# A constant guard column in the softmax's scores, with other due times for the planner

## The chip, the cores and the metric

One core of a Trainium2 chip runs the whole program in one launch. The metric is device time in microseconds (us), the median of several runs. TensorE (PE in the profile) multiplies matrices, VectorE (DVE), ScalarE (ACT) and GpSimd (POOL) work on tiles in on-chip memory, and SyncE (SP) issues nearly all the transfers (DMAs).

## The reference

What is computed is local attention followed by two layers of products. Cut to what matters:

```python
# attention: B=2, H=8, S=768, D=64; window of 16 to either side, and 24 summaries of 32 keys each
k_sum = k.reshape(B, H, nb, block, D).max(axis=3)
v_sum = v.reshape(B, H, nb, block, D).mean(axis=3)
scores_all = concat([where(|i - j| < 16, scale * q k^T, -1e9), scale * q k_sum^T + log(32)])
scores_all = scores_all - max(scores_all)
a = exp(scores_all)
a = a / (sum(a) + 1e-09)
x = a @ concat([v, v_sum])                      # 1536 x 512
h = ((x @ w1) * (x @ w2)) @ w3 @ w_out          # 1536 x 512
u = h @ w_in                                    # 1536 x 2048
y = (u * clip(u + 3, 0, 6) / 6) @ w_out2        # 1536 x 512
```

The addition of 1e-09 to the sum is the guard that the title speaks of.

## The kernel before, in words

**The products.** Every 32-bit operand is split into a high and a low part (`to_hi_lo`, lines 296 to 306: ACT writes the high part in line 301, POOL or DVE the low part in line 304), and a product is three matmuls (`products`, line 347): high by high, low by high, high by low. The weights arrive as 64-bit numbers; `to_f32` (lines 255 to 294) makes 32-bit ones of them with two operations on ACT or one on ACT and one on DVE (lines 277, 283, 288) and one more on DVE (line 292). `convert` (line 308) does both for one block of weights and numbers its calls; for the numbers in `LO_DVE` the low part is made on DVE, for all others on POOL. It is called 24 times for W' = w3 w_out (`wprime`: numbers 0 and 1 for the first step, 2 and 3 for the second, up to 15; then 16 to 23) and 16 times for w1 and w2 (numbers 24 to 39). Later weights go through `convert_out` and `w_in_group`, which count on but don't look at `LO_DVE`.

**The attention.** Queries are handled in 12 units u of two tiles of 64 queries each. `probabilities(u)` loads the queries, takes the scores on PE (line 483), and then: two DVE operations scale them and add the mask into the tile `sc` (line 493, 128 partitions, 8 groups of 120 scores each); DVE takes the maximum of each group into `st` (line 507); POOL subtracts it (line 509); ACT takes the exponential over all 960 elements (line 510); DVE sums each group (line 513), adds 1e-9 (line 514) and takes the reciprocal (line 515); POOL multiplies by it (line 519). `attend(u)` transposes the result on PE (line 529), copies it out, multiplies by the values on PE (line 544) and splits the result for the products. Units 0 to 3 make up the first block of 512 tokens; they read keys that stay on the chip (`kres`), and the summaries of the keys (`ksum`, three reductions on DVE, line 364) and of the values (`vsum`, three on DVE, line 400). The four transposes of `vsum` (`vsum_rows`, line 426) need the constants `con` for their identity matrix and go through bank 7 of the accumulator, which ACT empties (line 431); the scores of unit 0 use banks 6 and 7 after that.

**The order.** Nothing is issued in program order. Each piece of work is entered in `Graph` with its engine, an assumed duration and a due time. `schedule` first works the due times backwards: that of a PE operation is the least of its own and of what its users need, and that of an operation on any other engine comes from its users alone (its own is not read):

```python
due = [o[2] if o[0] == "pe" else self.LAST for o in self.ops]
for i in range(n - 1, -1, -1):
    for u in users[i]:
        e = self.ops[i][0]
        due[i] = min(due[i], due[u] - self.ops[i][1] - self.LAT.get(e, 40))
```

Then it runs a list schedule with the assumed durations: an engine that is free takes the ready operation that is due first. The result is a fixed order for each engine's queue. `slack` delays when the users of an operation count as ready, and `begin` when the operation itself may start. The constants on lines 157 to 172 feed this: `DUE_W` and `DUE_Q` for PE's W' products and attention units, `DUE_ROWS` for the transposes of `vsum`, `DUE_FF` for the start T1 of the main products, `AHEAD` for how far the later attention units stand ahead of them, `HOLD` for the slack of the late weights, `OUT_AT` for when the late weights may begin to load.

**The late stage.** From about the middle on, weights of the last layer are combined, spilled to DRAM (line 318) and fetched again (lines 322, 985, 1034), all by SP's queue; ACT copies results out of the accumulator (line 855).

Of the kernel before, what the change touches and what calls it, by code (L numbers as in the profile page):

```python
# [22 lines left out]
F32 = mybir.dt.float32  # L23
# [3 lines left out]
AF = mybir.ActivationFunctionType  # L27
ALU = mybir.AluOpType
AX = mybir.AxisListType

P = 128
# [9 lines left out]
NK = NWIN + NSUM  # L41
KW = 2 * QT + 2 * WIN
KS = KW + 2 * NSUM
NPAIR = H // 2
# [109 lines left out]

DUE_W = ((77.78, -6.43), (102.28, 1.95))
DUE_K, DUE_V, DUE_ROWS = 121.82, -109.4, 7.92
DUE_Q = (307.31, 41.78)
V_AT = 1  # L160
LO_DVE = [2, 9, 15, 16, 17, 18, 22, 26, 28, 29, 30, 31, 32, 36, 38, 42, 44, 45, 47]
L3_ACT = [2, 3, 4, 5, 6, 7, 8, 10, 11, 12, 15, 17, 18, 20, 22, 23, 24]
DUE_FF = 30.71
AHEAD, BEHIND = -16.03, -118.65
SUMS_AT, SUMS_DUE = 3, 5.0
POOL_MAX = ()
HOLD = 3512.7
SUMS_LATER = 22839.1
OUT_LATER = 31254.19
IN_AT = (8, 12)  # L170
LAST_ORDER = (0, 1, 4, 5, 2, 3, 6, 7)
OUT_AT, OUT_STEP = 174.13, 5.88


def build(tc, qd, kw, vw, kt, vt, consts, wp_in, w12_in, w2_in, out):
    nc = tc.nc
    g = Graph()
    us = 1000.0
# [4 lines left out]
    pool = main.__enter__()  # L183
# [13 lines left out]
    bank = [pp.tile([P, TB], F32, name=f"bank{i}") for i in range(8)]  # L197
# [7 lines left out]
    att = att_cm.__enter__()  # L205
    kall = [att.tile([P, NPAIR, KS], F32, name=f"kall{i}") for i in range(2)]
    vall = [att.tile([P, DM], F32, name=f"vall{i}") for i in range(4)]
    qst = [att.tile([P, 2, NPAIR, QT], F32, name=f"qst{i}") for i in range(2)]
    sc = [att.tile([P, 2, NPAIR, NK], F32, name=f"sc{i}") for i in range(2)]
    pt = [att.tile([P, NPAIR * P], F32, name=f"pt{i}") for i in range(2)]  # L210
    st = [att.tile([P, 3, 2 * NPAIR], F32, name=f"st{i}") for i in range(2)]
    con = att.tile([P, 4 * NK + P], F32, name="con")
# [2 lines left out]
    ident = con[:, 4 * NK :]  # L215
# [140 lines left out]

    load(0, lambda: con, consts, P * (4 * NK + P) * 4, ["con"])
    g.op("pool", 60, 0, lambda: nc.gpsimd.memset(three, 3.0), (), ["three"])


    def max32(due, x, c, reads):
# [88 lines left out]
    def probabilities(u, due, bk):  # L450
        i2, uu = u % 2, u % PPB
        ki, si, sti, qs = kall[i2], sc[i2], st[i2], qst[i2]
# [36 lines left out]
        for x in range(2):  # L489
            m = (0 if uu == 0 else 1) if x == 0 else (3 if uu == PPB - 1 else 2)  # L490
            g.op(
                "dve", 660, due + 1 * us,
                lambda x=x, m=m: nc.vector.scalar_tensor_tensor(  # L493
                    out=si[:, x], in0=bank[bk[x]][:, 0 : NPAIR * NK].rearrange("p (a n) -> p a n", a=NPAIR),
                    scalar=SCALE, in1=con[:, m * NK : (m + 1) * NK].unsqueeze(1).to_broadcast((P, NPAIR, NK)),
                    op0=ALU.mult, op1=ALU.add,
                ), [("bank", bk[x]), "con"], [("s", i2, x)],
            )
        s8 = si.rearrange("p x a n -> p (x a) n")
        s1 = si.rearrange("p x a n -> p (x a n)")  # L500
        skeys = [("s", i2, 0), ("s", i2, 1)]

        def wide(k):
# [3 lines left out]
             lambda: nc.vector.tensor_reduce(out=sti[:, 0, :], in_=s8, op=ALU.max, axis=AX.X), skeys, [("st", i2)])  # L507
        g.op("pool", 2000, due + 3 * us,
             lambda: nc.gpsimd.tensor_tensor(out=s8, in0=s8, in1=wide(0), op=ALU.subtract), [("st", i2)], skeys)  # L509
        g.op("act", 1020, due + 4 * us, lambda: nc.scalar.activation(out=s1, in_=s1, func=AF.Exp), [], skeys)  # L510

        def inv():
            nc.vector.tensor_reduce(out=sti[:, 2, :], in_=s8, op=ALU.add, axis=AX.X)
            nc.vector.tensor_scalar(out=sti[:, 0, :], in0=sti[:, 2, :], scalar1=1e-9, scalar2=None, op0=ALU.add)
            nc.vector.reciprocal(out=sti[:, 1, :], in_=sti[:, 0, :])  # L515

        g.op("dve", 1560, due + 5 * us, inv, skeys, [("st", i2)])
        g.op("pool", 2000, due + 5.5 * us,
             lambda: nc.gpsimd.tensor_tensor(out=s8, in0=s8, in1=wide(1), op=ALU.mult), [("st", i2)], skeys)  # L519

    def attend(u, due, b0, b1):
        i2 = u % 2
        j, col = u // PPK, (u % PPK) * 2 * QT
        s0 = A_X + NPAIR * j
        si, vi, bk = sc[i2], [2 * i2, 2 * i2 + 1], (b0, b1)

        def trans(x):
            for p in range(NPAIR):
                nc.tensor.transpose(bank[bk[x]][0:NK, p * P : (p + 1) * P], si[:, x, p, :], ident)  # L529

        for x in range(2):
            g.op("pe", 480, due + 7 * us, lambda x=x: trans(x), [("s", i2, x), "con"], [("bank", bk[x])])
# [148 lines left out]
    with tc.manual_schedule():  # L681
        first_k(DUE_K * us)
        for n in range(2 * NFC):
            if n < NFC:
                wprime(0, n, (DUE_W[0][0] + DUE_W[0][1] * n) * us)
            else:
                wprime(1, n - NFC, (DUE_W[1][0] + DUE_W[1][1] * (n - NFC)) * us)
            if n == V_AT:
# [9 lines left out]
        for u in range(PPK):  # L698
            at = (DUE_Q[0] + DUE_Q[1] * u) * us
            probabilities(u, at, (6, 7))  # L700
# [26 lines left out]
        due = T1  # L727
        pend = None
        for j in range(NBLK):
            for n_i in range(NFC):  # L730
                i = LAST_ORDER[n_i] if j == NBLK - 1 else n_i
# [284 lines left out]
        for n, store, i, hh, bks, start in LAST:  # L1016
            last = n == LAST[-1][0]
            done = []
            for k in range(NFC):
                b11, b21, b12, b22 = held(k), moved(0, 1, k), moved(1, 0, k), moved(1, 1, k)  # L1020
                other = (lambda k=k: tmps[6 + k % 2]), ("f", 6 + k % 2)
                o, x, y = {
                    1: (b11, None, None), 2: (b21, None, None), 3: (b22, None, None),
                    5: (b11, b12, b11), 6: (b11, b22, b11), 7: (other, b22, b12), 4: (other, b21, b11),
                }[n]
                if x:
                    tensors(due, o[0], x[0], y[0], ALU.subtract, x[1], y[1], o[1], "dve")
                s = t_ring[n_t % len(t_ring)]
# [6 lines left out]
                         out=slot(ws)[:, wh, :].bitcast(F32).rearrange("p (two n) -> p two n", two=2),  # L1035
                         in_=d[:, :, hh * H : (hh + 1) * H]),
                     [(store, 2 * k + i)], [("t", ws, wh)])
                done.append((s, ws, wh))
                for m in range(2):
                    if last and k >= NFC - 3:  # L1040
                        continue
                    terms = [(lambda a, ws=ws, wh=wh, m=m: slot(ws)[:, wh, a * H + m * P : a * H + (m + 1) * P],
                              lambda c, s=s: slot(s)[:, c, :])]
# [3 lines left out]
            for m in range(2):  # L1047
                if last:
                    for s, ws, wh in done[NFC - 3 :]:
                        terms = [(lambda a, ws=ws, wh=wh, m=m: slot(ws)[:, wh, a * H + m * P : a * H + (m + 1) * P],  # L1050
                                  lambda c, s=s: slot(s)[:, c, :])]
# [91 lines left out]
```

## Time and profile before

| | |
|---|---|
| median of 3 runs | 557.11 us (555.17 to 557.39) |
| the profiled execution | 555.27 us |
| its span, first to last instruction | 553.5 us |
| PE busy in it | 526.9 us (95%) |
| DVE, ACT, POOL busy | 375.7, 303.5, 289.2 us |
| mean granted TensorE clock | 0.99 |

A row of a timeline gives start, duration, engine, line, operation and tiles, and in brackets how long the engine had been idle before it and what ended that. The chain of waits follows the work that ended last back to the start. "x32" is a number of instructions merged in one row.

### The profile page before, as it was taken

What the parts mean: (1) busy time and instruction counts of PE and PEld (TensorE: products, weight loads), DVE (VectorE), ACT (ScalarE), POOL (GpSimd) and SP (SyncE); (2) the same over time, 40 slices, a digit from 0 to 9 for tenths busy, and PEclk for the clock granted to TensorE, in tenths of its full rate; (3) what the DMA queues carried; (4) which work ended last, traced back from release to release, by engine and by line L of the source; (5) the groups of instructions that cost most, each with busy time, mean ns of one, the idle gap of its engine ahead of it and who ended that gap; (6) DMA issues with size and microseconds to landing.
All of it is one profiled execution on the core that took longest, in us unless ns stands there. A gap on an engine that the chain in (4) does not pass through costs nothing.

```text
span 553.5 us, 8514 instructions
## 1 busy us (share of the span) xinstructions
PE 526.9 (95%) x3112; PEld 431.4 (78%) x3112; DVE 375.7 (68%) x460; ACT 303.5 (55%) x517; POOL 289.2 (52%) x239
## 2 busy tenths in 40 slices
PE   0399999999999999999999999999999999999997
PEld 0388788888788888888888888888888887888875
DVE  5889978578463447777553866577775569689941
ACT  0879876484232446564545786655663456734630
POOL 0668454673221334374728665875785563644630
PEclk9789999999999999999999999999999999999999
DMA  8999678662241368633347576475444679877631
GB/s 318 363 364 336 197 245 261 187 195 62 65 123 53 121 215 270 218 115 115 114 157 229 222 247 209 156 263 172 150 174 142 209 264 366 294 256 231 190 103 75
DMA packets 54513, 111.32 MB, mean 201 GB/s; under 512 B 4792, under 2 KB 26296, under 8 KB 54472
## 3 DMA queue, kind: packets, MB, share of 16 engines
q1 hardware_dynamic: 54472, 110.79, 59.9%
q8 instruction: 24, 0.39, 0.3%
q14 instruction: 17, 0.14, 0.1%
HBM read 84.26 MB, written 26.21 MB: 200 GB/s over the span
## 4 chain that ended last, share of the span: by engine, by line
PE 91%; DMA 4%; DVE 1%; SPq 1%; POOL 1%; issue 0%; ACT 0%; ACTq 0%; DVEq 0%
PE bank L347 84%; PE bank L544 2%; PE bank L483 2%; PE bank L529 2%; DMA con<-in_con_dram 2%; DMA ws<-arena 1%; DMA w<-wo 1%; SPq L249 1%; DMA gj<-tg 1%; DVE sc L493 0%; POOL sc L519 0%; POOL sc L509 0%; SPq L1034 0%; PE bank L426 0%; DVE st L507 0%
## 5 line engine op out<-in xcount | busy, mean ns | idle before, releaser
L347 PE MATMUL bank<-arena,w 128*128 128x512 f32 x1152 | 268.3, 390 | 1.2 <-ACT late_f L855 1.2
L347 PEld LDWEIGHTS bank<-arena,w 128*128 128x128 f32 x1152 | 215.4, 188 | 47.2 <-ACT late_f L855 2.4
L347 PE MATMUL bank<-arena 128*128 128x512 f32 x960 | 230.9, 394 | 0.0
L347 PEld LDWEIGHTS bank<-arena 128*128 128x128 f32 x960 | 178.8, 189 | 38.2 <-issue 0.8
L292 DVE SCALAR_TENSOR_TENSOR c<-c,raw 128x512 uint32<-128x512 uint32 x48 | 47.7, 1006 | 22.2 <-ACT raw L283 17.5
L301 ACT ACTIVATE arena<-late_f 128x512 fp32r<-128x512 f32 x64 | 39.5, 628 | 39.2 <-DVE late_f L770 16.8
L304 POOL TENSOR_TENSOR w<-c,w 128x512 fp32r<-128x512 f32 x29 | 44.0, 1525 | 24.4 <-ACT w L301 24.3
L304 DVE TENSOR_TENSOR arena<-late_f,arena 128x512 fp32r<-128x512 f32 x44 | 39.6, 901 | 20.5 <-ACT arena L301 20.2
L826 POOL TENSOR_TENSOR late_f<-arena 128x512 f32<-128x512 f32 x16 | 23.2, 1447 | 44.7 <-DMA arena<-wo 30.4
L304 POOL TENSOR_TENSOR arena<-late_f,arena 128x512 fp32r<-128x512 f32 x20 | 29.5, 1476 | 32.0 <-ACT arena L301 26.5
L277 ACT ACTIVATE c<-raw 128x512 f32<-128x512 f32 x48 | 31.6, 663 | 25.2 <-DMA raw<-in_w_dram 24.3
L283 ACT ACTIVATE raw<-raw 128x512 uint32<-128x512 uint32 (+1 forms) x66 | 42.9, 655 | 0.0
L598 DVE TENSOR_TENSOR tg<-ta,bank 128x512 f32<-128x512 f32 x24 | 16.5, 685 | 38.8 <-PE bank L347 33.0
L304 POOL TENSOR_TENSOR raw<-c,raw 128x512 fp32r<-128x512 f32 x16 | 21.7, 1360 | 40.3 <-ACT raw L301 38.8
L509 POOL TENSOR_TENSOR sc<-sc,st 128x960 f32<-128x960 f32 x12 | 23.5, 1957 | 31.5 <-DVE st L507 31.5
L579 DVE TENSOR_TENSOR arena<-tg,arena 128x512 fp32r<-128x512 f32 x36 | 34.4, 955 | 5.4 <-ACT arena L574 4.8
L304 POOL TENSOR_TENSOR arena<-c,arena 128x512 fp32r<-128x512 f32 (+1 forms) x22 | 27.0, 1243 | 20.6 <-ACT arena L301 20.5
L574 ACT ACTIVATE arena<-tg 128x512 fp32r<-128x512 f32 x40 | 25.2, 629 | 20.1 <-DVE tg L598 16.6
L874 DVE SCALAR_TENSOR_TENSOR late_f<-ta,late_f 128x512 f32<-128x512 f32 x24 | 28.9, 1204 | 6.7 <-ACT ta L871 6.3
L770 DVE TENSOR_TENSOR late_f<-arena,late_f 128x512 f32<-128x512 f32 x24 | 29.1, 1242 | 6.2 <-DMA arena<-gj 6.1
L301 ACT ACTIVATE w<-c 128x512 fp32r<-128x512 f32 x40 | 24.6, 625 | 14.8 <-POOL c L770 6.5
L519 POOL TENSOR_TENSOR sc<-sc,st 128x960 f32<-128x960 f32 x12 | 22.0, 1832 | 17.0 <-DVE st L515 16.6
(68 smaller groups left out, 553.4 us busy)
## 6 DMA issues: line engine op xcount, KB each, us to landing
raw<-in_w_dram SPq DMA_DIRECT2D x48, 512.0 KB, 4.7
raw<-in_wp_dram SPq DMA_DIRECT2D x22, 512.0 KB, 6.0
wo<-raw SPq DMA_DIRECT2D x16, 512.0 KB, 3.4
arena<-wo SPq DMA_DIRECT2D x16, 512.0 KB, 3.3
ws<-arena SPq DMA_DIRECT2D x16, 512.0 KB, 3.4
w<-ws SPq DMA_DIRECT2D x32, 256.0 KB, 4.0
arena<-gj SPq DMA_DIRECT2D x24, 256.0 KB, 4.5
w<-wo SPq DMA_DIRECT2D x24, 256.0 KB, 4.0
```

The costliest lines, as they stand in the source:

```text
L277: lambda uf=uf, wf=wf: nc.scalar.activation(out=uf, in_=wf[:, :, 1], func=AF.Prelu, scale=2.0**-112, alpha=-(2.0**32)),
L283: lambda lw=lw: nc.scalar.activation(out=lw, in_=lw, func=AF.Copy, scale=2.0**-29 * (1 - eps), bias=7.5 * eps - 0.5),
L292: lambda ci=ci, ui=ui, lw=lw: nc.vector.scalar_tensor_tensor(out=ci, in0=ui, scalar=3, in1=lw, op0=ALU.logical_shift_left, op1=ALU.bitwise ...
L301: lambda: nc.scalar.activation(out=hi(), in_=src(), func=AF.Copy), keys, khi)
L304: lambda: e.tensor_tensor(out=lo(), in0=src(), in1=hi().bitcast(F32), op=ALU.subtract),
L347: nc.tensor.matmul(out=out_ap, lhsT=lhs(a), rhs=rhs(c), start=start and n == 0, stop=stop and n == 3 * len(terms) - 1, skip_group_check=skip,)
L509: lambda: nc.gpsimd.tensor_tensor(out=s8, in0=s8, in1=wide(0), op=ALU.subtract), [("st", i2)], skeys)
L574: g.op("act", 630, due, lambda: nc.scalar.activation(out=slot(s)[:, 0, :], in_=src_ap, func=AF.Copy), [src_key], [("t", s, 0)])
L579: lambda: eng.tensor_tensor(out=slot(s)[:, 1, :], in0=src_ap, in1=slot(s)[:, 0, :].bitcast(F32), op=ALU.subtract), [src_key, ("t", s, 0)], ...
L770: lambda: e.tensor_tensor(out=out(), in0=a(), in1=b(), op=op), [ka, kb], [ko], True)
L826: lambda i=i, s=s: nc.gpsimd.tensor_tensor(out=tmps[6 + i], in0=f32s(s, 0)(), in1=f32s(s, 1)(), op=ALU.add), both(s), [k])
L874: lambda: nc.vector.scalar_tensor_tensor(out=dst(), in0=t, scalar=6.0, in1=h(), op0=ALU.min, op1=ALU.mult),
```

## The change

The score tile gets a 121st column in each group. It is set to 1e-9 once for each of the two buffers by POOL, before any unit, and no later operation writes it. Scaling, maximum, subtraction, exponential and multiplication work on the first 120 columns; the sum takes all 121, and so holds the guard already. The separate addition goes. The exponential, which ran over 960 elements in a row, now runs over 8 groups of 120 with a gap of one. The assumed duration of the sum and reciprocal falls from 1560 to 1420 ns. The planner's constants change too.

```diff
-DUE_W = ((77.78, -6.43), (102.28, 1.95))
-DUE_K, DUE_V, DUE_ROWS = 121.82, -109.4, 7.92
-DUE_Q = (307.31, 41.78)
+DUE_W = ((77.78, -6.43), (139.42, 1.95))
+DUE_K, DUE_V, DUE_ROWS = 121.82, -109.4, -31.56
+DUE_Q = (309.83, 41.78)
-LO_DVE = [2, 9, 15, 16, 17, 18, 22, 26, 28, 29, 30, 31, 32, 36, 38, 42, 44, 45, 47]
+LO_DVE = [9, 13, 16, 17, 18, 22, 26, 28, 29, 30, 31, 32, 38, 42, 44, 47]
-DUE_FF = 30.71
-AHEAD, BEHIND = -16.03, -118.65
+DUE_FF = 31.07
+AHEAD, BEHIND = -15.06, -118.65
-HOLD = 3512.7
+HOLD = 3470.14
-OUT_LATER = 31254.19
+OUT_LATER = 33015.51
-OUT_AT, OUT_STEP = 174.13, 5.88
+OUT_AT, OUT_STEP = 174.69, 5.88
...
-    sc = [att.tile([P, 2, NPAIR, NK], F32, name=f"sc{i}") for i in range(2)]
+    sc = [att.tile([P, 2, NPAIR, NK + 1], F32, name=f"sc{i}") for i in range(2)]
...
+    for i in range(2):
+        g.op("pool", 60, 0,
+             lambda i=i: nc.gpsimd.memset(sc[i].rearrange("p x a n -> p (x a) n")[:, :, NK : NK + 1], 1e-9),
+             (), [("s", i, x) for x in range(2)])
...
-        s8 = si.rearrange("p x a n -> p (x a) n")
-        s1 = si.rearrange("p x a n -> p (x a n)")
+        all8 = si.rearrange("p x a n -> p (x a) n")
+        s8 = all8[:, :, 0:NK]
...
-        g.op("act", 1020, due + 4 * us, lambda: nc.scalar.activation(out=s1, in_=s1, func=AF.Exp), [], skeys)
+        g.op("act", 1020, due + 4 * us, lambda: nc.scalar.activation(out=s8, in_=s8, func=AF.Exp), [], skeys)
...
-            nc.vector.tensor_reduce(out=sti[:, 2, :], in_=s8, op=ALU.add, axis=AX.X)
-            nc.vector.tensor_scalar(out=sti[:, 0, :], in0=sti[:, 2, :], scalar1=1e-9, scalar2=None, op0=ALU.add)
-            nc.vector.reciprocal(out=sti[:, 1, :], in_=sti[:, 0, :])
-        g.op("dve", 1560, due + 5 * us, inv, skeys, [("st", i2)])
+            nc.vector.tensor_reduce(out=sti[:, 2, :], in_=all8, op=ALU.add, axis=AX.X)
+            nc.vector.reciprocal(out=sti[:, 1, :], in_=sti[:, 2, :])
+        g.op("dve", 1420, due + 5 * us, inv, skeys, [("st", i2)])
```

In `probabilities` and `attend` the writes of the scores (line 493) and the reads of the transposes (line 529) name the first 120 columns in the same way.

## Rows read from the trace of the kernel before

**Rows 1.** The page's first part: busy time, share of the span, instructions of each engine.
```profile
PE 526.9 (95%) x3112; PEld 431.4 (78%) x3112; DVE 375.7 (68%) x460; ACT 303.5 (55%) x517; POOL 289.2 (52%) x239
```

**Rows 2.** The waits of PE: engine, line, released by, us in total, times, longest.
```profile
PE bank L426 <- DMA con<-in_con_dram: 13.1, 1, 13.1
PE bank L529 <- POOL sc L519: 7.0, 1, 7.0
PE bank L483 <- DVE sc L493: 1.3, 1, 1.3
PE bank L347 <- ACT late_f L855: 1.2, 1, 1.2
```

**Rows 3.** Windows: stretch, its length, busy us (count) by engine, PE's clock, DMA share, GB/s.
```profile
19.81:26.84 7.03, 0.00 (x1) 0.00 (x1) 6.37 (x11) 6.98 (x13) 5.84 (x5) 0.54 0.98 327
26.84:32.16 5.32, 5.32 (x47) 4.50 (x47) 4.09 (x7) 3.23 (x6) 5.16 (x4) 0.65 1.02 397
```

**Rows 4.** The chain of waits: start, us, what. Its beginning, and two late pieces.
```profile
4.27 8.65 DMA con<-in_con_dram
...
13.05 1.03 PE bank L426 x4
14.10 0.60 ACT vall L431
14.74 2.24 PE bank L483 x34
...
24.34 0.31 POOL arena L304
...
24.99 1.80 POOL sc L519
...
454.17 6.22 DMA ws<-arena
...
461.64 54.74 PE bank L347 x240
```

**Rows 5.** The timeline of SP's queue in the first 5 us: the order of the loads.
```profile
0.73 0.86 SPq L249 DMA_DIRECT2D raw<-in_vt_dram  x2
1.64 0.65 SPq L249 DMA_DIRECT2D kres<-in_kt_dram  x1
2.33 0.61 SPq L249 DMA_DIRECT2D raw<-in_vt_dram  x1
2.98 1.24 SPq L249 DMA_DIRECT2D kres<-in_kt_dram  x2
4.27 0.91 SPq L249 DMA_DIRECT2D con<-in_con_dram  x1
```

**Rows 6.** The timeline of DVE: the last key reduction, and unit 0's guard and reciprocal.
```profile
12.17 1.22 DVE L364 TENSOR_REDUCE ksum<-kres 128x32 f32<-128x1024 f32 x1 [0.25 <-DMA kres<-in_kt_dram]
...
24.16 0.20 DVE L514 TENSOR_SCALAR st<-st 128x8 f32<-128x8 f32 x1
24.40 0.20 DVE L515 RECIPROCAL st<-st 128x8 f32<-128x8 f32 x1
```

**Rows 7.** The guard's own line, all 12: duration ns least/median/most, first and last start.
```profile
L514 DVE TENSOR_SCALAR st<-st x12: 171/188/1184, 24.2 to 232.3; 128x8 f32<-128x8 f32 x12
```

**Rows 8.** Groups by line and form: POOL additions on 512 elements, flat and strided.
```profile
L304 POOL TENSOR_TENSOR arena<-c,arena 128x512 fp32r<-128x512 f32 x18 | 24.2, 1356 | 18.4 <-ACT arena L301 18.3
L378 POOL TENSOR_TENSOR raw<-raw 128x512 f32<-128x512 f32 x3 | 4.7, 1570 | 0.1
```

**Rows 9.** The timeline of POOL where the last W' blocks of the first half are split.
```profile
51.32 2.54 POOL L304 TENSOR_TENSOR arena<-c,arena 128x512 fp32r<-128x512 f32 x2
53.82 2.24 POOL L509 TENSOR_TENSOR sc<-sc,st 128x960 f32<-128x960 f32 x1
62.59 1.30 POOL L304 TENSOR_TENSOR arena<-c,arena 128x512 fp32r<-128x512 f32 x1 [6.53 <-ACT arena L301]
```

**Rows 10.** The timeline of SP's queue ahead of the late spill.
```profile
450.25 3.56 SPq L985 DMA_DIRECT2D arena<-gj  x5
```

More of the change, by code (lines that the diff above doesn't have):

```diff
@@ L493, in probabilities @@
                 lambda x=x, m=m: nc.vector.scalar_tensor_tensor(
-                    out=si[:, x], in0=bank[bk[x]][:, 0 : NPAIR * NK].rearrange("p (a n) -> p a n", a=NPAIR),
+                    out=si[:, x, :, 0:NK], in0=bank[bk[x]][:, 0 : NPAIR * NK].rearrange("p (a n) -> p a n", a=NPAIR),
                     scalar=SCALE, in1=con[:, m * NK : (m + 1) * NK].unsqueeze(1).to_broadcast((P, NPAIR, NK)),
@@ L528, in trans @@
             for p in range(NPAIR):
-                nc.tensor.transpose(bank[bk[x]][0:NK, p * P : (p + 1) * P], si[:, x, p, :], ident)
+                nc.tensor.transpose(bank[bk[x]][0:NK, p * P : (p + 1) * P], si[:, x, p, 0:NK], ident)
         for x in range(2):
```

## The prediction

> **What bounds the kernel now.** I began with the busy line of the page: PE is busy for 526.9 of 553.5 us [rows 1], so at most 26.6 us can be had without giving PE less to do, and the change takes nothing from PE. Next the waits of PE, which say where those 26.6 us are: 13.1 until the constants have landed, 7.0 until unit 0's softmax is done, 1.3 in between, and 1.2 once late, on a copy by ACT [rows 2]. They make 22.8; the rest is mostly the end, after the last matmul. So PE stops only ahead of 26.84 us and once near 461 us. Between these it works without a gap, and an operation of DVE or POOL there costs or saves nothing until it is late enough to stop PE. The reader should see from this that 11 of the 12 softmaxes are hidden: only unit 0's is on the path.
>
> Then the windows around the first softmax: in 19.81 to 26.84 PE runs nothing and its granted clock averages 0.54, that is, it has dropped to its lower level (1.2 GHz); in the next 5.32 us it averages 0.65 [rows 3]. Beginning earlier by a fraction of a microsecond leaves such a pause and its slow restart as they are, so the stretch behind it moves as a whole. Last, the chain of waits through the start [rows 4], and the queues that feed it [rows 5, 6].
>
> **Start: the order of the loads.** A PE operation's due time counts, and others take theirs from their users. The planner's backward pass gives the transposes of `vsum` an inherited due time of -6.43 us before the change (arithmetic of the listing, no time of the chip), so their own 7.92 didn't count. The new -31.56 does, and with it the three V loads and `con` become due before the keys' loads. The queue now has V, V, K, V, K, K, con [rows 5]; I expect V, V, V, con, K, K, K. It is the same set of bytes, so the last of the seven should land when `con` does now, at 4.27 + 8.65 = 12.92 [rows 4]. Before, what followed was transposes from 13.05 (1.03), ACT's copy from 14.10 (0.60), scores at 14.74 [rows 4]. After, the transposes and the copy run while the keys still arrive, and the last key load is followed by one reduction of 1.22 [rows 6] alone: 12.92 + 1.22 = 14.14, scores at about 14.19 with the hand-over. Gain 14.74 - 14.19 = 0.55 us. The ends: if the last key block still landed for a reduction at 12.17 [rows 6], the scores could start at 13.39 + 0.05, a gain of 1.3; if it came one reduction (1.22) later than I say, a loss of 0.67. I take 0.55, the value that the bytes give.
>
> **Unit 0's softmax: the guard goes.** From the start of the guard to the start of the reciprocal are 24.40 - 24.16 = 0.24 us [rows 6]. That would be the gain if POOL were waiting. It isn't: a low part (line 304) stands in its queue in front of the multiplication and the multiplication starts at 24.99 [rows 4], 0.39 us after the reciprocal's end at 24.60. I count the 0.24 as covered: 0. If the planner puts that low part behind the multiplication, POOL starts at 24.36 and the gain is 24.99 - 24.36 = 0.63. The assumed duration falls by only 0.14, so I keep the order as it is and 0.63 for the range.
>
> **The other eleven guards.** They take 0.17 to 1.18 us each [rows 7], some six times the shortest at worst. Under the PE work of the middle they are hidden; gain 0. It is a reserve for DVE, not time.
>
> **The 121st column.** The sum takes 8 more elements of 968; at the 1.22 us of 1024 elements [rows 6] that is 10 ns. POOL's two passes and ACT's exponential now walk rows 121 apart. No row shows this form. The nearest pair: POOL on 512 elements takes 1356 ns flat and 1570 strided, with groups of 16 out of 32 [rows 8], 16% more. On unit 0's path one POOL pass of 1.80 [rows 4] would then gain 0.28, two 0.57; the lower end is 0, since the broadcast operand made POOL walk 8 rows already. A gain is excluded, as no element is saved. I take 0: rows of 120 with a gap of one are much nearer to flat.
>
> The Trainium skill speaks against this column: in "SBUF — State Buffer", section "Door 1: The DMA port swizzle", it says that this memory has lines of 16 bytes and each access that crosses to a new line pays. Rows of 480 bytes begin on a line; of those of 484 only every fourth does, and the other 120-element rows touch 31 lines in place of 30. By that rule a pass of 1.80 grows by 0.06 at most, two by 0.12, and the sum below would be -0.43 where I have -0.55; no row here shows lines.
>
> **Two memsets** of 8 elements on POOL at the very start: what waits for them follows the first scores, which end at 14.74 + 2.24 = 16.98 [rows 4]. Cost 0; without that cover I would put them at 0.2 each, an estimate from DVE's 0.20 for 8 elements [rows 6].
>
> **Low parts that change engines.** Only numbers up to 39 are looked up, so what changes is 2, 15 and 36 from DVE to POOL and 13 from POOL to DVE. One costs POOL 1.36 us [rows 8]. Number 2 falls in a stretch in which POOL works 5.16 of 5.32 us [rows 3]; queued behind it is unit 1's multiplication, which PE needs only after several W' products. Number 15 falls behind the pair at 51.32 and ahead of unit 3's subtraction (2.24), after which POOL is idle for 6.53 us [rows 9]; number 13, which POOL loses in front of it, pays for it. Number 36 falls where PE has long blocks ahead. Each 0; without cover number 15 would hold PE by up to 1.36.
>
> **The other constants.** The second W' due time and `DUE_Q` stand later than what their users ask for, before and after: nothing. `OUT_LATER` goes to no PE operation and isn't read. T1 moves by 0.36 with everything behind it; `AHEAD` puts the later units 0.97 us earlier against the products, which PE does back to back in either order. `OUT_AT` and `HOLD` let the late weights load 0.5 us later. What this could touch is the late wait of 1.2 us [rows 2]. Ends: the wait gone (-1.2), or the slower rival below. I take 0.
>
> **The sum**: -0.55 + 0 = -0.55 us. The profiled execution took 555.27 (span 553.5 and 1.77 around it), which would become 554.7. The median of the runs shown is 557.11, 1.84 above the profiled one; I forecast the median: 557.11 - 0.55 = 556.6. A measurement of this kernel can tell about 0.5%, 2.8 us, from no change.
>
> **The rivals.** (a) *The load order changes nothing.* The chain has other steps that wait for weights: DVE and ACT take weight operations between unit 0's steps, and if these hold the softmax at the same time as before, an earlier start of the scores is lost in front of them. For it: the DMA share is 0.98 up to 26.84 [rows 3]; against it: unit 0's steps in the chain follow each other closely. This is also the case in which the planner doesn't move the loads. Time 557.1.
>
> (b) *Faster: PE's 7.0 us are filled.* If the new plan lets the first W' products run before unit 0's transposes, 12 matmuls leave the path behind. At 54.74 / 240 = 0.228 us each [rows 4] that is 2.7, with the load order 3.3: 553.8. Against it: the last low part of the first step comes on POOL only behind unit 0's multiplication, and a shorter softmax makes the transposes earlier still.
>
> (c) *Slower: the late hand-over.* PE's wait near 461 us ends a chain through a spill that takes 454.17 to 460.39 [rows 4] and that SP issues behind five fetches, whose issue alone takes 3.56 us [rows 10]. If the shifted late weights make the planner put five more fetches ahead of that spill, it lands 3.56 later, the slot comes free later, and PE, which has no cover there (it waits already), stands for all of it: 557.11 - 0.55 + 3.56 = 560.1. It decides from 3.35 us on, at 559.9. For it: the queue is full of fetches of nearly the same due time. Against it: the shift is 0.5 us, less than one of these.
>
> **How the numbers follow.** The forecast has 0.53: the start gains something, the rest holds. Its own range is from -1.3 - 0.63 - 1.2 = -3.1 (554.0) to +0.67 + 0.57 = +1.2 (558.3). (a) has 0.20, within it. (b) has 0.13, (c) 0.14. Faster by over 0.5% (below 554.3) is (b) and a little of the low end of the forecast, 0.17; slower (above 559.9) is (c), 0.14; no difference 0.69. The range goes from just under (b), 553.5, to 559.4, short of (c).
>
> **What would show it.** Right: SP issues V, V, V, con, K, K, K; PE's first wait ends well before 13 us and another small one, on the keys' reduction, stands before the scores; scores begin near 14.2; unit 0's transposes begin at 26.3 in place of 26.84; PE busy unchanged; line 514 gone and DVE's total less by some 5 us. Wrong: a new wait of PE between 27 and 440 us (POOL low parts too late, above all number 15), a late wait other than 1.2, POOL's two passes of unit 0 over 1.80, or PE products before unit 0's transposes.

## The result: 0.5% slower, by loads that stand behind a waiting queue entry

The changed kernel took 559.31 us (median of 8 runs, 557.43 to 561.63), the kernel before 556.70 beside it (8 runs, 554.88 to 557.86): a ratio of 1.0051, with a 95% interval of 1.0029 to 1.0074. I had forecast 556.6, a small gain. The time lies in the range given, 0.1 us from its upper end of 559.4, but its sign is the other one. That it lies there is luck: no term of the range stood for what took the time, and a second measurement of the same kernel, e8 below, gives 560.20. The profiled execution took 558.5 us, its span 556.7, 3.2 longer than before.

The page's busy line answers [rows 1], and PE's waits answer [rows 2]:

```profile
PE 527.8 (95%) x3112; PEld 431.7 (78%) x3112; DVE 369.6 (66%) x446; ACT 301.3 (54%) x517; POOL 290.5 (52%) x243
```

```profile
PE bank L430 <- DVE vsum L404: 8.5, 1, 8.5
PE bank L532 <- POOL sc L522: 7.3, 2, 6.8
PE bank L487 <- DMA qst<-in_q_dram: 5.9, 2, 3.8
PE bank L347 <- ACT late_f L858: 2.0, 2, 1.5
PE bank L532 <- DVE sc L497: 1.4, 1, 1.4
```

DVE lost 6.1 us of work and the time did not fall: the guards were hidden. The start is cut up in another way: 8.5 + 6.8 + 5.9 = 21.2 us of waits, where it had 13.1 + 7.0 + 1.3 = 21.4. New are 1.4 us for the scores of line 497, a second wait of 0.5 (7.3 less 6.8) for line 522, and a second one for `late_f`.

**The start** changed in its order as forecast, and gained nothing. SP's queue (compare [rows 5]):

```profile
0.74 1.34 SPq L249 DMA_DIRECT2D raw<-in_vt_dram  x3
2.12 0.43 SPq L249 DMA_DIRECT2D con<-in_con_dram  x1
2.60 2.08 SPq L249 DMA_DIRECT2D kres<-in_kt_dram  x3
```

The beginning of the chain of waits (compare [rows 4]):

```profile
3.29 7.69 DMA kres<-in_kt_dram
...
11.00 6.82 DMA qst<-in_q_dram
...
17.96 2.35 PE bank L487 x56
...
20.32 1.23 DVE sc L497 x2
...
21.58 1.16 DVE st L511
...
22.81 1.79 POOL sc L513
24.61 0.65 POOL arena L304
25.26 1.80 POOL sc L522
```

These scores are unit 1's, not unit 0's. Unit 0's ran from 13.28 to 15.81 us, where before four of them ran at 14.00 and the rest from 14.74 to 16.98 [rows 4]. But what the chain goes through now are unit 1's queries, which take 6.82 us to land, then unit 1's scores, maximum and subtraction. Unit 0's sum and multiplication stand behind these in the queues of DVE and POOL. So its transposes begin at 27.10 (26.84 before), and the product of unit 3 ends at 71.74 us (71.71 before). The start is worth 0.

**The middle** is where the time went. Three rows of PE's timeline after the change, and below them one of before that answers to the last:

```profile
227.67 1.13 PE L532 MATMUL bank<-con,sc 128*120 128x128 f32 x8 [1.39 <-DVE sc L497]
...
238.14 1.09 PE L532 MATMUL bank<-con,sc 128*120 128x128 f32 x8 [0.55 <-POOL sc L522]
...
242.34 3.04 PE L347 MATMUL bank<-arena 128*128 128x512 f32 x12
```

```profile
239.87 5.51 PE L347 MATMUL bank<-arena 128*128 128x512 f32 x23
```

PE's first matmul behind the last unit's product starts 2.47 us later than before; 1.39 + 0.55 = 1.94 of it are the two waits. What the first of them waits for shows in DVE's timeline: DVE stands idle for ACT ahead of two weight operations, and the scaling of unit 11's scores (line 497), which frees the banks that PE needs, stands behind them.

```profile
223.25 0.69 DVE L292 SCALAR_TENSOR_TENSOR c<-c,raw 128x512 uint32<-128x512 uint32 x1 [4.34 <-ACT raw L283]
225.67 0.69 DVE L292 SCALAR_TENSOR_TENSOR c<-c,raw 128x512 uint32<-128x512 uint32 x1 [1.73 <-ACT raw L283]
...
226.88 1.22 DVE L497 SCALAR_TENSOR_TENSOR sc<-bank,con 128x480 f32<-128x480 f32 x2
```

Before, this scaling began at 224.65. ACT in its turn waited for the weights, and SP's queue says why these were late. Before, then after the change:

```profile
208.47 0.32 SPq L318 DMA_DIRECT2D wo<-raw  x1
211.49 0.81 SPq L249 DMA_DIRECT2D raw<-in_w_dram  x2
212.46 0.80 SPq L249 DMA_DIRECT2D vall<-in_vw_dram  x2
```

```profile
209.78 0.81 SPq L249 DMA_DIRECT2D vall<-in_vw_dram  x2
210.67 0.38 SPq L249 DMA_DIRECT2D raw<-in_w_dram  x1
212.27 0.34 SPq L318 DMA_DIRECT2D wo<-raw  x1
217.71 0.33 SPq L249 DMA_DIRECT2D raw<-in_w_dram  x1
```

The two `vall<-in_vw_dram` are unit 11's windows of the values. They overwrite what unit 9's product (line 547) reads, so they can't be issued before it ends, at 209.8. Before, one spill and two weight loads stood ahead of them and went out from 208.47 on. Now the windows stand ahead and the queue waits on them until 209.78. The spill goes out at 212.27, 3.8 us later than before. The next load reuses the buffer that the spill reads, so it waits until the spill has landed, at 217.71: 5.4 us behind the spill's start, where it was 3.0 (211.49). The windows and a load of 512 KB now go out just ahead of that spill; in e5, e8 and e11 below, where they do so too, it is 4.8 to 6.2, in e9 and e13, where they don't, 2.7 and 3.0.

The spill waited for a second thing, POOL's low part. Before, then after the change:

```profile
207.16 1.29 POOL L304 TENSOR_TENSOR raw<-c,raw 128x512 fp32r<-128x512 f32 x1 [1.73 <-ACT raw L301]
```

```profile
210.94 1.30 POOL L304 TENSOR_TENSOR raw<-c,raw 128x512 fp32r<-128x512 f32 x1
```

It ends at 212.24 and stands behind unit 10's subtraction now (208.90, line 513); before, it was done ahead of it. So two queues hold the spill in the changed kernel, SP's and POOL's; e11 and e13 take them apart.

**The late stage** adds the rest: two pieces at the end of the chain are

```profile
464.52 53.35 PE bank L347 x234
...
519.67 11.18 PE bank L347 x48
```

The first answers the hand-over at 461.64 [rows 4]. Of its delay, 2.47 come from the middle; its own wait grew from 1.16 to 1.55, and the one ahead of 519.67 is new (0.45). 2.47 + 0.39 + 0.45 = 3.3, the 3.2 of the span. Waits of this kind come and go between kernels that are equally fast (e1 and e12 below have 1.8 and 1.5 us of them), so I count the middle alone as the change's. From the start of unit 11's product on, the profiled executions of all kernels here take 313.9 to 315.5 us (before: 314.7, changed: 315.5).

### The profile page after: what moved, and what is told of

Read it like the earlier page. It is cut to its first block, busy times and chain, and to the rows that moved or that the text cites. A ratio compares the mean times of both kernels' runs of the same rounds, so it can differ in the third digit from the quotient of the medians.

```text
span 556.7 us, 8505 instructions
## 1 busy us (share of the span) xinstructions
PE 527.8 (95%) x3112; PEld 431.7 (78%) x3112; DVE 369.6 (66%) x446; ACT 301.3 (54%) x517; POOL 290.5 (52%) x243
## 4 chain that ended last, share of the span: by engine, by line
PE 86%; DMA 7%; POOL 2%; DVE 2%; ACT 1%; issue 1%; SPq 1%; POOLq 0%; ACTq 0%
PE bank L347 80%; PE bank L487 2%; PE bank L547 2%; PE bank L532 2%; DMA kres<-in_kt_dram 1%; DMA qst<-in_q_dram 1%; DMA ws<-arena 1%; DMA raw<-in_w_dram 1%; DMA w<-wo 1%; DMA wo<-raw 1%; POOL sc L513 1%; POOL sc L522 1%; DVE st L511 1%; SPq L249 0%; DVE sc L497 0%
## 5 line engine op out<-in xcount | busy, mean ns | idle before, releaser
L292 DVE SCALAR_TENSOR_TENSOR c<-c,raw 128x512 uint32<-128x512 uint32 x48 | 45.9, 969 | 28.4 <-ACT raw L283 27.8
L304 POOL TENSOR_TENSOR w<-c,w 128x512 fp32r<-128x512 f32 x30 | 45.8, 1535 | 20.4 <-ACT w L301 20.2
L304 DVE TENSOR_TENSOR arena<-late_f,arena 128x512 fp32r<-128x512 f32 x44 | 42.5, 967 | 19.0 <-ACT arena L301 18.9
L513 POOL TENSOR_TENSOR sc<-sc,st 128x960 f32<-128x960 f32 x12 | 23.5, 1958 | 39.0 <-DVE st L511 39.0
L582 DVE TENSOR_TENSOR arena<-tg,arena 128x512 fp32r<-128x512 f32 x36 | 32.1, 891 | 7.3 <-ACT arena L577 6.5
L877 DVE SCALAR_TENSOR_TENSOR late_f<-ta,late_f 128x512 f32<-128x512 f32 x24 | 30.9, 1288 | 6.1 <-ACT ta L874 5.8
L773 DVE TENSOR_TENSOR late_f<-arena,late_f 128x512 f32<-128x512 f32 x24 | 27.9, 1192 | 5.9 <-DMA arena<-gj 5.8
L599 ACT ACTIVATE ta<-bank 128x512 f32<-128x512 f32 x24 | 14.2, 594 | 31.0 <-PE bank L347 31.0
```

The source lines that it names most:

```text
L292: lambda ci=ci, ui=ui, lw=lw: nc.vector.scalar_tensor_tensor(out=ci, in0=ui, scalar=3, in1=lw, op0=ALU.logical_shift_left, op1=ALU.bitwise ...
L304: lambda: e.tensor_tensor(out=lo(), in0=src(), in1=hi().bitcast(F32), op=ALU.subtract),
L582: lambda: eng.tensor_tensor(out=slot(s)[:, 1, :], in0=src_ap, in1=slot(s)[:, 0, :].bitcast(F32), op=ALU.subtract), [src_key, ("t", s, 0)], ...
L773: lambda: e.tensor_tensor(out=out(), in0=a(), in1=b(), op=op), [ka, kb], [ko], True)
L877: lambda: nc.vector.scalar_tensor_tensor(out=dst(), in0=t, scalar=6.0, in1=h(), op0=ALU.min, op1=ALU.mult),
```

## The experiments

Each ratio is against the kernel before, in 5 rounds on the same chip. "Changed" and "before" say which kernel the edit starts from.

| | kernel | us | ratio, 95% interval | PE's waits from 200 to 245 us |
|---|---|---|---|---|
| e8 | changed, again | 560.20 | 1.0067 [1.0041, 1.0092] | 0.98 and 0.61 |
| e1 | before + column | 557.05 | 1.0006 [0.9992, 1.0020] | none |
| e6 | before + `DUE_ROWS` | 556.71 | 0.9998 [0.9981, 1.0015] | none |
| e7 | before + `LO_DVE` | 557.10 | 1.0015 [0.9998, 1.0031] | 0.4 |
| e4 | before + `AHEAD` | 557.00 | 1.0014 [0.9997, 1.0031] | none |
| e5 | before + `OUT_AT`, `HOLD` | 564.76 | 1.0143 [1.0114, 1.0171] | 4.95 |
| e2 | changed, `AHEAD` back | 560.99 | 1.0081 [1.0050, 1.0111] | 1.8 |
| e3 | changed, `OUT_AT`, `HOLD` back | 557.86 | 1.0025 [1.0002, 1.0048] | none |
| e12 | changed, all three back | 557.07 | 1.0008 [0.9989, 1.0027] | none |
| e9 | e5, SP's order back | 557.54 | 1.0030 [1.0009, 1.0051] | 1.0 |
| e10 | e5, engines' order back | 563.70 | 1.0135 [1.0110, 1.0159] | 5.6 |
| e11 | changed, engines' order back | 560.82 | 1.0078 [1.0048, 1.0107] | 1.07 and 0.48 |
| e13 | e11, SP's order back too | 557.96 | 1.0022 [1.0003, 1.0040] | none |
| e14 | e12, unit 0's softmax first | 559.39 | 1.0051 [1.0031, 1.0070] | none |
| e15 | e14, its copies first too | 556.98 | 1.0015 [0.9994, 1.0037] | none |

### Which part costs the time

**e1**, the column and nothing else, with the assumed duration as before, so that the order of all queues is as before (its edit against the changed kernel):

```diff
-DUE_W = ((77.78, -6.43), (139.42, 1.95))
+DUE_W = ((77.78, -6.43), (102.28, 1.95))
...
-        g.op("dve", 1420, due + 5 * us, inv, skeys, [("st", i2)])
+        g.op("dve", 1560, due + 5 * us, inv, skeys, [("st", i2)])
```

(and every other constant as before).

> Column of 121 and no guard addition, but the planner's constants and the assumed 1560 ns of the kernel before, which give every queue the order of the kernel before. Theory (the order of the queues costs the time, the column itself does nothing or saves a little): 0 to -0.5 us against before; no wait of PE between 30 and 440 us; PE's wait for unit 0's softmax 7.0 or up to 0.3 shorter. Rival (the column makes the softmax's passes slow): +2 us or more, POOL's passes of lines 513 and 522 over 1.80 us, and the wait for unit 0 longer by 0.3 or more.

Measured: 1.0006. Its interval goes from 0.9992 to 1.0020, so the column gains no more than 0.5 and costs no more than 1.1 us. PE's wait for unit 0's softmax is 7.0 again: the guard was covered.

**e2**: the changed kernel with

```diff
-AHEAD, BEHIND = -15.06, -118.65
+AHEAD, BEHIND = -16.03, -118.65
```

> The changed kernel with AHEAD at -16.03 as before and all else as changed. Theory (AHEAD puts the transposes of the later units ahead of the second group of products, where PE meets a softmax or a bank that isn't free): PE's waits near 227 (1.4 us) and 238 us (0.55) vanish, the time falls by about 1.9 us against the changed kernel, to about +1 us against before. Rival (the late loads, moved by OUT_AT, hold up DVE whatever PE's order is): the waits move or stay, and the time stays within 0.5 us of the changed kernel's +2.9.

**e3**: the changed kernel with

```diff
-HOLD = 3470.14
+HOLD = 3512.7
-OUT_AT, OUT_STEP = 174.69, 5.88
+OUT_AT, OUT_STEP = 174.13, 5.88
```

> The changed kernel with OUT_AT 174.13 and HOLD 3512.7 as before and all else as changed. Theory (AHEAD is the cause): the wait near 227 us stays, though it may be shorter; time within 1 us of the changed kernel's +2.9 against before. Rival (the late loads are the cause): the waits near 227 and 238 us vanish, and the late wait near 460 us is 1.2 again and not 2.0; the time falls by about 2.7 us, to about 0 against before.

**e4**: `AHEAD` alone, the reverse of e2's lines, in the kernel before.

> The kernel before with AHEAD at -15.06 and nothing else changed. Theory (AHEAD alone brings the waits): PE waits between 200 and 240 us by 1 to 2 us in all, time +1 to +2 us against before. Rival (AHEAD costs only together with later loads): no wait there over 0.3 us, time within 0.7 us of before.

My first suspect was `AHEAD`, since the wait at 227.67 stands at transposes that it put behind 6 products instead of 12. That fell: taken back (e2) it leaves 1.0081, alone (e4) it costs 1.0014 with an interval that holds 1. Taking the late loads back (e3) removes much of the loss: 1.0025, and PE has no wait left between 200 and 245 us. Its interval still overlaps the changed kernel's; with `AHEAD` back as well (e12 below) it is 1.0008. In e3 and e4 the transposes of the fifth unit, near 110 us, wait 1.42 and 0.64 us for line 497 (493), which no profile without the new `AHEAD` shows (the changed kernel's own two have none and 0.54): this may be the small rest. The runs of e2 go from 558.77 to 564.34, and the profiled one is the fastest of them, so its trace doesn't show all of what e2 loses.

**e5**: the two late constants alone, the reverse of e3's lines, in the kernel before.

> The kernel before with OUT_AT 174.69 and HOLD 3470.14 and nothing else changed. Theory (the late loads' new place in SP's queue, behind a unit's value windows, is one of the causes): +0.5 to +1.5 us against before, with a wait of PE between 200 and 245 us or a longer one near 460 us. Rival (it takes the earlier transposes too): within 0.5 us of before, PE's order being the same, and no PE wait between 116 and 440 us.

Measured: 1.0143, 8.0 us, far over the 0.5 to 1.5 expected and nearly three times what the whole change costs. SP, DVE and PE in e5:

```profile
214.42 0.80 SPq L249 DMA_DIRECT2D vall<-in_vw_dram  x2
...
215.78 0.39 SPq L318 DMA_DIRECT2D wo<-raw  x1
```

```profile
231.95 0.69 DVE L292 SCALAR_TENSOR_TENSOR c<-c,raw 128x512 uint32<-128x512 uint32 x1 [3.13 <-ACT raw L283]
...
233.15 1.22 DVE L493 SCALAR_TENSOR_TENSOR sc<-bank,con 128x480 f32<-128x480 f32 x2
```

```profile
234.51 1.93 PE L529 MATMUL bank<-con,sc 128*120 128x128 f32 x8 [4.95 <-DVE sc L493]
236.10 4.72 PE L347 MATMUL bank<-arena,w 128*128 128x512 f32 x12
```

It is the changed kernel's picture, later: here unit 9's product ends only at 214.4, so the windows hold the queue until 214.42, against 209.78. Some 2 us of that this execution had lost before 137 us; the other 2.7 are the changed kernel's earlier product (208.70, before 211.38). The wait's price is more than the 4.95 us: the matmuls behind the pause run slowly (1.93 for the 8 transposes, where the kernel before needs 1.03, and 4.72 for 12, where it needs 2.98). 4.95 + 0.90 + 1.74 = 7.6, nearly all of the 8.0.

Why the two late constants cost 8.0 us alone and less in the whole change isn't settled. The earlier product lets the windows go sooner, but `AHEAD` doesn't bring it by itself: in e4 unit 9's product starts 50.38 us behind unit 7's, as before (50.41), and in the changed kernel 47.70. And e2, which lacks it too, is at 1.0081 and not at 1.0143; there one of three entries, a weight load, goes out near 206, ahead of the windows.

**e6** and **e7**: `DUE_ROWS` alone and `LO_DVE` alone, in the kernel before.

```diff
-DUE_K, DUE_V, DUE_ROWS = 121.82, -109.4, 7.92
+DUE_K, DUE_V, DUE_ROWS = 121.82, -109.4, -31.56
```

> The kernel before with DUE_ROWS at -31.56 and nothing else changed: the values' loads and the constants go ahead of the keys'. Theory (the start gives nothing, since unit 1's queries land last and the softmax of unit 0 waits behind unit 1's subtraction on POOL): unit 0's scores begin near 13.3 us, unit 1's near 18.0, unit 0's transposes between 26.6 and 27.4; time within 0.7 us of before. Rival (my forecast): transposes near 26.3 and -0.5 us.

```diff
-LO_DVE = [2, 9, 15, 16, 17, 18, 22, 26, 28, 29, 30, 31, 32, 36, 38, 42, 44, 45, 47]
+LO_DVE = [9, 13, 16, 17, 18, 22, 26, 28, 29, 30, 31, 32, 38, 42, 44, 47]
```

> The kernel before with the new LO_DVE and nothing else changed: low parts 2, 15 and 36 on POOL, 13 on DVE. Theory (POOL and DVE have room for it): within 0.5 us of before. Rival (POOL is late for the W' products or the first main products): a wait of PE between 30 and 120 us on POOL L304 or behind it, +0.7 us or more.

Both intervals hold 1. In e6 unit 0's transposes begin at 27.34 although its scores begin nearly as early as in the changed kernel (13.52): the start gains nothing by the loads alone. In e7 PE doesn't wait between 30 and 120 us, so the low part number 15, which I had feared, stayed hidden.

**e8**: the changed kernel once more, unedited, for its spread.

> The changed kernel once more, beside these. Theory (its waits belong to its order of queues): +2 to +3.5 us against before, and again waits of PE between 105 and 240 us of 1 to 2.5 us in all, on DVE L497, POOL L522 or POOL L304. Rival (the waits of the first profile were chance): none over 0.5 us there, with the time lost elsewhere.

Measured 1.0067 beside 1.0051; the waits near 228 and 239 us are there again (0.98 and 0.61).

### Which queue carries it

The two late constants, which no run separates, move several things at once: in SP's queue the spill and two loads, and on ACT, DVE and POOL the operations of the late block ahead of that spill. A few lines in the loop that issues the plan put single entries back, with the same constants:

```diff
-        for _, i in g.schedule():
+        order = [i for _, i in g.schedule()]
+        for early, ahead in [(941, 724), (933, 724), (955, 724)]:
+            order.remove(early)
+            order.insert(order.index(ahead), early)
+        for i in order:
             g.ops[i][3]()
```

This is **e9**, from e5: load 941, spill 933 and load 955 ahead of the value windows 724 and 725.

> The kernel of e5 with three of SP's entries ahead of unit 11's two value windows again (a late load, a spill, the next late load); all other queues as in e5. Theory (SP stands still on the value windows, which wait for unit 9's product until 214.4 us, and the spill and the late loads stand behind them): the spill goes out near 213.3, when POOL has its low part, in place of 215.8, what hangs on it comes 2.5 us earlier or more; PE's wait of 4.9 us near 234 falls to 2.5 or less; time +2 to +5.5 us against before where e5 has +8. Rival (the order on ACT, DVE and POOL is what delays the block): the wait stays over 4 us and the time within 1 us of e5's.

**e10**, from e5 as well, moves the late block's operations on ACT, DVE and POOL ahead of unit 10's softmax and leaves SP alone:

```diff
+        for early, ahead in [(928, 716), (929, 716), (930, 689), (931, 691), (932, 691)]:
```

> The kernel of e5 with one late block's five operations on ACT, DVE and POOL ahead of unit 10's softmax again; SP's order as in e5. Theory (SP's order is the first bound): POOL has the low part some 3 to 5 us earlier, but the spill still goes out only near 215.8; PE's wait near 234 stays between 4 and 5.5 us, time within 1 us of e5's +8. Rival (engine order): the wait falls under 2.5 us, time +5 or less.

e9 takes the ratio from 1.0143 to 1.0030; e10 leaves it at 1.0135. In e10 the low part that the spill waits for is done at 208.98 us, and the spill still goes out at 215.48 only. In e9 it goes out ahead of the windows:

```profile
211.67 0.33 SPq L318 DMA_DIRECT2D wo<-raw  x1
...
214.72 0.89 SPq L249 DMA_DIRECT2D vall<-in_vw_dram  x2
```

So in e5 it is SP's queue: three entries of it cost some 6.3 us, and the engines' order by itself nothing that shows.

**e11** does in the changed kernel what e10 does in e5, with the last three of its five operations (word, high part, low part), and **e13** adds SP's order (the numbers are higher by 2, for the two memsets):

```diff
+        for early, ahead in [(932, 691), (933, 698), (934, 693)]:
```

> The changed kernel with the same late block's operations on DVE, ACT and POOL (word, high part, low part) ahead of unit 10's softmax again; SP's order and all else as changed. Theory (here unit 9's product is 2.7 us earlier, SP waits only until 209.8, and the spill waits for POOL's low part): the spill goes out near 211 in place of 212.3, PE's wait near 228 falls from 1.0 to 1.4 to under 0.4, time 1 to 2 us less than the changed kernel's. Rival (the waits near 228 and 239 come from the earlier transposes alone): the same waits, time within 0.5 us of the changed kernel's.

```diff
+        for early, ahead in [(932, 691), (933, 698), (934, 693), (943, 726), (935, 726), (957, 726)]:
```

> The changed kernel with the one late block's three operations on ACT, DVE and POOL ahead of unit 10's softmax (as in e11), and now also SP's queue as before the change: that block's spill and the two late weight loads stand ahead of unit 11's two value windows. All else as changed. Theory (SP's queue stands still on the value windows; the late loads behind them set the loss between 190 and 245 us): the spill is issued before 210 us, the waits of PE between 200 and 245 us shrink to under 0.5 together, the matmuls of the last unit end by 240.5 instead of 242.4, and the ratio falls from 1.005 to 1.008 to 1.002 or less, 557.0 to 558.0. Rival (AHEAD's order of the transposes costs the time by itself, whatever SP's queue holds): waits near 228 us stay at 1 us, ratio 1.005 or more, 559.5.

**e12**: the changed kernel with the edits of e2 and e3 together.

> The changed kernel with AHEAD, OUT_AT and HOLD as before; the column, the load order at the start and the low parts as changed. Theory (late loads and AHEAD make the loss; the rest is 0.06, 0 and 0.15% as measured alone): +0 to +1.5 us against before, no PE wait over 0.5 us between 200 and 245 us. Rival (the rest costs more together than alone): +2 us or more.

e11 stays at 1.0078 (its runs go from 558.58 to 563.37). POOL's low part is done at 208.84 there, and yet the spill goes out at 212.65 only, behind the windows, which wait until 211.28. I had expected a gain; what came are the numbers of its rival, that the earlier transposes alone make the waits. e13 refutes that rival: with the same transposes and SP's order back, the spill goes out at 210.07, PE has no wait between 200 and 245 us, and the ratio falls to 1.0022, with an interval that doesn't meet e11's. SP's order alone wasn't put back in the changed kernel, where the low part is done at 212.24 only; so that it would do by itself there isn't shown.

Behind the start e13 has two waits of PE, 1.24 at the fifth unit (109.69) and 1.2 on `late_f`. The end of the last unit's product was expected by 240.5 and came at 242.69: unit 3's product ends 0.9 us later than in the changed kernel, and the wait at 109.69 follows, so the absolute time misses, while the stretch from 200 on is clean.

One stretch shows what these edits give back. From the start of unit 7's product (line 544 or 547) to that of unit 11's PE takes 77.82 us before (160.97 to 238.79), 80.25 in the changed kernel (161.00 to 241.25), 79.89 in e8 and 79.85 in e11, but 77.83 in e13 and 77.82 in e3; in e5 it is 85.50, in e9 79.03. So 2.1 to 2.4 of the 2.8 and 3.7 us that the two measurements of the changed kernel give lie there; where the others are lost isn't shown.

e12, without the new `AHEAD` and without the late constants, is at 1.0008: what is left of the change, the column, the loads' order, the low parts and the other due times, costs nothing that shows. The rest of 0.1 to 0.2% in e3, e4 and e13 goes with `AHEAD`; their intervals overlap e12's, so that this rest is `AHEAD`'s isn't shown.

### What the start could have been worth

**e14**, from e12: unit 0's exponential, sum and multiplication (270 to 272) ahead of unit 1's maximum (279), and two small low parts with their ACT operations ahead of unit 1's subtraction (280).

```diff
+        for early, ahead in [(270, 279), (271, 279), (272, 279), (32, 280), (33, 280), (20, 280), (21, 280)]:
```

> The kernel of e12 (the change, with AHEAD, OUT_AT and HOLD as before it), with unit 0's sum and reciprocal on DVE ahead of unit 1's maximum, unit 0's multiplication on POOL ahead of unit 1's subtraction, and the two low parts of the first weights directly behind it. Theory (the earlier scores of unit 0 are lost because unit 1's steps, and a low part, stand ahead of unit 0's sum and multiplication): the sum begins near 22.0 instead of 23.3, unit 0's transposes begin at 25.2 to 25.5 instead of 27.2, and what follows moves with them: 555.2 to 556.0, ratio 0.996 to 0.998. Rival (the first weights' transfers or the low parts bind the first products, so that earlier transposes only end earlier): transposes near 25.3 as well, but the first products no earlier than 28.5 and PE at 71.7 us where it was; 557.0, ratio 1.000 to 1.001.

The transposes begin at 25.51 as expected, 1.7 us before e12's, and the time is worse, 1.0051, which neither the theory nor its rival had. One step further on there is a new wait:

```profile
29.66 1.16 DVE L517 TENSOR_REDUCE st<-sc 128x8 f32<-128x968 f32 x1 [3.92 <-ACT sc L514]
```

```profile
32.30 1.98 PE L547 MATMUL bank<-pt,vall 120*64 120x64 f32 x32 [2.27 <-ACT pt L539]
...
34.21 4.07 PE L347 MATMUL bank<-arena 128*128 128x512 f32 x9
```

The first row is unit 1's sum on DVE, which now comes later (its exponential on ACT too); unit 0's copies stand behind these, DVE's at 31.54. PE waits 2.27 for ACT's copy, and 9 matmuls behind the pause take 4.07 us (e12: 2.34).

**e15**, from e14: the transposes and their two copies (285 and 287) ahead of unit 1's exponential as well.

```diff
+        for early, ahead in [..., (286, 281), (284, 281), (285, 281), (287, 281)]:
```

> The kernel of e14, and unit 0's two copies of the transposes (DVE and ACT) ahead of unit 1's sum and exponential, behind which they stood. Theory (e14's loss is a new pause of PE of 2.27 us before unit 0's product, because these copies stood behind unit 1's steps, and the slower matmuls behind that pause): no wait of PE between 26 and 80 us, unit 0's product ends by 32.3, the product of unit 3 ends near 70 instead of 71.7 (e12), 555.3 to 556.2 us, ratio 0.997 to 0.999 (0.9965 if all 1.7 us of the earlier transposes stay). Rival (unit 1's softmax, now later, or the weights' low parts behind it are late next): a pause of PE between 32 and 42 us, 557 to 559, ratio 1.001 to 1.005.

PE in e12 and then in e15:

```profile
27.23 1.96 PE L532 MATMUL bank<-con,sc 128*120 128x128 f32 x8 [6.80 <-POOL sc L522]
28.84 2.22 PE L347 MATMUL bank<-arena 128*128 128x512 f32 x6
...
34.34 0.40 PE L487 MATMUL bank<-kres,qst 64*64 64x96 f32 x8
```

```profile
24.86 1.96 PE L532 MATMUL bank<-con,sc 128*120 128x128 f32 x8 [4.86 <-POOL sc L522]
26.48 2.91 PE L347 MATMUL bank<-arena 128*128 128x512 f32 x6
29.31 1.62 PE L547 MATMUL bank<-pt,vall 120*64 120x64 f32 x32
...
34.03 0.40 PE L487 MATMUL bank<-kres,qst 64*64 64x96 f32 x8 [0.80 <-DVE arena L564]
```

2.37 us earlier at the transposes, 0.31 at the next scores: 0.69 go to the first six matmuls and 0.47 to the product (1.62, in e12 1.15), which run longer, and 0.80 to a new wait for line 564. 1.0015, no gain that shows. The rival that I had named (weights or unit 1's steps late next) holds: in the first 35 us each step that came sooner uncovered the next. No version here is clear of the noise faster than the kernel before.

## Why the prediction was wrong

*What bounds the kernel* was right: the guards that DVE no longer does and the memsets moved nothing (e1), and the only way to lose time in the middle was a new wait of PE, which came. (The four waits of [rows 2] make 22.6 us, not 22.8, and the guard's longest run is nearly seven times its shortest; nothing hangs on either.)

*Start: the order of the loads* (0.55). The order was right to the entry. The scores gained more than I said, 1.17 us at their end: the keys' reductions ended at 13.73, not 14.14, the first matmuls didn't wait for them but for unit 0's queries, and unit 0's maximum, subtraction and exponential all ran 0.77 earlier (exponential at 20.77, 21.54 before). Then it was lost in one place: its sum came at 23.25, before at 22.99, behind unit 1's scaling, maximum and a weight operation on DVE. These hang on unit 1's scores, whose queries land at 17.82 only and which take 2.35 us in place of the 1.44 from 18.37 to 19.81. The chain of before had gone through unit 1 already, in pieces that I left out of [rows 4]:

```profile
20.16 1.14 DVE sc L493 x2
...
22.55 1.79 POOL sc L509
```

These are unit 1's scaling and subtraction. The sentence "unit 0's steps in the chain follow each other closely" was a misreading of it: in this order of the queues an earlier unit 0 is worth something only as far as unit 1 comes earlier too. This is what rival (a) said (other work ahead of unit 0's steps), though I had looked for weights there and not for unit 1. The term measured 0: unit 3's product ends where it did. e14 and e15, which move unit 0's steps ahead of unit 1's, gain nothing either.

*Guard of unit 0*: 0, right, and for the reason given. In the changed kernel POOL's low part runs from 24.56 to 25.26, across the reciprocal's end at 24.63. *The column*: 0, right. The durations (least/median/most, ns) of POOL's multiplication, before and after:

```profile
L519 POOL TENSOR_TENSOR sc<-sc,st x12: 1792/1793/2255, 25.0 to 232.9; 128x960 f32<-128x960 f32 x12
```

```profile
L522 POOL TENSOR_TENSOR sc<-sc,st x12: 1792/1794/2240, 25.3 to 236.3; 128x960 f32<-128x960 f32 x12
```

Rows of 484 bytes cost POOL 1 ns at the median. The growth of 0.06 us that I worked out from the Trainium skill's lines of 16 bytes ("SBUF — State Buffer", "Door 1: The DMA port swizzle") isn't seen; the measurement decides. *Low parts*: 0, right (e7).

*The other constants* is the step that failed, with the sentence "`OUT_AT` and `HOLD` let the late weights load 0.5 us later. What this could touch is the late wait of 1.2 us". I costed the time at which loads may begin by its shift. What it did was to let two entries that wait pass three others in SP's queue, 250 us before the place I looked at. Alone it costs 8.0 us (e5), in the whole change, together with the low part behind unit 10's subtraction, the larger part of 2.8 and 3.7 (0.51% and 0.67% in the two measurements of the changed kernel). `AHEAD`, "which PE does back to back in either order", also wasn't free of effect: alone it moves unit 8's product 2.7 us earlier (e4), with the late constants unit 9's too, and with it what the windows wait for.

*Rival (c)* was near the mechanism, a spill held up in SP's queue by entries ahead of it, and nearly the price (3.56). Its place was wrong: I looked near 461 us because PE waited there already. I had weighed five fetches at 0.7 us each, and not entries that wait themselves: those hold the queue for as long as what they wait for is late. A case of its kind deserved more than 0.14 in a plan that makes every queue anew.

## What to carry to other kernels

A planner's constant that shifts by half a microsecond is costed by the order that it makes, not by the shift: list each queue's entries before and after, and look first at a transfer that waits for an engine's work and at what now stands behind it. Where a queue is served in order, such an entry belongs behind all that can go out already. And a step on the critical path is worth only what the next queue lets through: ask for each step whose work stands ahead of it, and what sets the start of that.

## What was not expected of the hardware

The granted clock and the durations disagree. In the changed kernel PE pauses for 6.79 us and the windows show full clock in the pause and behind it:

```profile
20.31:27.10 6.79, 0.00 (x0) 0.00 (x0) 6.06 (x9) 6.03 (x11) 4.56 (x5) 1.00 1.03 366
27.10:32.43 5.33, 5.33 (x47) 4.57 (x48) 2.00 (x4) 3.22 (x7) 5.33 (x5) 1.00 0.95 354
```

Yet six matmuls behind that pause take 2.41 us, 0.40 each, where 240 late ones take 0.228 each [rows 4]; in [rows 3] the same pause shows 0.54 and 0.65. The Trainium skill ("TensorE: Matmul & The Clock Gate", "Seeing it yourself") says that such clock events have been seen to be unreliable on this chip. This case agrees, in that two profiles show 0.54 and 1.00 for a like pause, with matmuls about as slow behind both (2.62 us for the six before the change). The level (1.2 or 2.4 GHz) is better read from the durations.
